# Fewer, longer butterfly operations and a new order of the work beside the matmuls, in a two-part kernel (attention with memory, and a spectral filter)

## The chip, the core and the metric

The kernel runs on one core of one Trainium2 chip, as one program. A core has a matrix engine (PE, with its weight loads shown apart as PEld), a vector engine (DVE), a scalar engine (ACT), a general engine (POOL), and queues that issue transfers between main memory and the core's own memory (SP's queue, POOL's queue). Each engine executes its instructions in the order in which they stand and waits for the others by semaphores. The metric is the device time of one execution in microseconds (us).

## The reference

Two independent computations share the launch and their results are laid side by side.

Part A is attention with a compressive memory: 2048 rows, 576 columns, 32 heads of 18, four segments of 512 rows.

```python
q, k, v = heads(x @ wq), heads(x @ wk), heads(x @ wv)
for s in range(4):                                   # segments
    logits = einsum("hqd,hkd->hqk", q_s, k_s) * 18**-0.5 + causal_mask
    a_dot  = softmax(logits) @ v_s
    a_mem  = (phi(q_s) @ M) / (phi(q_s) @ z + 1e-6)  # phi(t) = t+1 if t>0 else exp(t)
    out_s  = g * a_mem + (1 - g) * a_dot             # g = sigmoid(beta), per head
    M, z   = M + phi(k_s).T @ v_s, z + phi(k_s).sum(rows)
a = concat(out) @ wo
```

Part B filters a real 2048 x 576 array in the frequency domain:

```python
X = rfft2(x)                    # 2048 x 289 complex
b = irfft2(X * (w_r + 1j * w_i))
```

## The kernel before, in words

All matmuls of float32 data are done as three products of rounded halves (high x high, high x low, low x high), so every operand is first split: ACT copies the rounded high half, DVE (or POOL) subtracts it and writes the low half. The program goes through five stages.

1. **Forward transform** (`FFT.forward`, iterations u = 0 to 19, 16 blocks of 128 rows). `prep(u+2)` forms sums and differences of a block (`eo`, DVE, line 125), their high half `eh` (ACT, line 127) and low half `el` (DVE, lines 131 and 132). `f1(u)` transforms along the columns (PE, line 142). `ev0` and `ev1` take the result from PSUM as a high half (ACT, line 146) and a low half (DVE, line 149). `c1(u-3)` transforms 128 points along the rows (PE, line 162, two PSUM tiles of tag "c1", of which there are two), and `evz` copies the result into `Z` one iteration later (ACT, line 153). `Z` is 128 x 4 x 4 x (real, imaginary) x 290: 16 complex rows per partition. Beside it run the splits of the weights of q and k (`load_w`, ACT line 403, DVE lines 405 and 406) and of the first 512 rows of part A's input (`xprep`, DVE lines 432 and 438).
2. **Projections** (`ATT.projections`). Four groups of 13 units: 9 units of q and k (128 output columns each, 14 matmuls of 128x512) and 4 units of v (28 of 128x288). Behind a q or k unit stands a chain: ACT copies the sums to bfloat16 (line 471), DVE subtracts (line 478), ACT copies again (line 482), and PE takes the second part out with a matmul by minus the identity (line 484) that stands in PE's order in the middle of the unit two later. Where phi is wanted, ACT computes exp (line 475) and DVE finishes phi (line 477).
3. **Inverse transform** (`FFT.inverse`, u = 0 to 17): `ysplit` splits the rows of `Z` into `Y` (ACT line 280, POOL or DVE line 281), `i2(u)` transforms along the rows (PE line 296), `T` is taken from PSUM (ACT line 326, DVE line 328), `i3` transforms along the columns (PE line 307). The maxima of the first ten attention heads (`s1`) run between.
4. **Attention** (133 steps), 5. the **last output projection**.

Between the row transforms of stages 1 and 3 the 16 complex rows of each partition go through a 16-point transform as two passes of four-point butterflies, a product with the filter, and the same back. This is all vector work on `Z`, without matmuls: `stage1` (butterfly `bf`, then rotations `tws`), `middle` (butterfly, product with `W`, inverse butterfly, rotations), `last` (inverse butterfly). A butterfly is ten DVE operations (line 206), six on a whole complex row (580 numbers) and four on half of one (290). A rotation is two ACT operations on whole rows (lines 216 and 217) and two DVE operations on halves (lines 222 and 224). The product with the filter is four DVE operations per row, two of them on halves (lines 245 to 252).

These steps stand in a list of generators, and a `Pace` object deals them out: `take(f)` adds f to an account and emits one step for each whole number in it. There are 61 + 165 + 40 = 266 steps. The forward loop takes one per iteration up to u = 13 and two after it (there is nothing to take before u = 7), the projections take a fixed share per unit, with 2.4 times as much in a v unit as in a q or k unit, 0.4 of it ahead of the second step of the earlier unit's chain (the one with line 478) and 0.6 behind it, and ten steps are left for the inverse transform. The order of everything is written out by hand in this way; no scheduler moves instructions.

## Time and profile before

| | |
|---|---|
| three runs | 734.36, 738.96, 740.35 us (median 738.96) |
| the profiled execution's own time | 736.84 us |
| its span, first to last instruction | 735.1 us |
| PE, DVE, ACT, POOL busy | 691.1, 553.4, 457.9, 204.2 us |
| mean granted clock of the matrix engine | 0.994 |

A busy matrix engine is not one at its peak: matmuls overlap, and their ends are modelled, so the distance between the starts of two matmuls says more than their durations. On DVE and ACT, too, an operation's duration is longer than the distance to the start of the next one, since the end of one overlaps the beginning of the next.

### The profile page before, as it was taken

The numbers are of one execution on the slowest core, as the hardware profiler recorded it, in microseconds if no ns is written. First come the engines' busy times: TensorE is split into PE (matmuls) and PEld (weight loads), VectorE is DVE, ScalarE is ACT, GpSimd is POOL, SyncE is SP. The second block draws the span as 40 slices with busy tenths as digits, with TensorE's granted clock in tenths as the row PEclk, the third lists the DMA queues.
The fourth block names the chain that finished last, engine by engine and source line by source line (L and its number), as shares of the span: only waits on it lengthen the run. The fifth ranks groups of instructions, "written<-read, shape, count | busy, mean of one in ns | idle before, by whom it ended". The sixth has DMA issues, their size and how long they took to land.

```text
span 735.1 us, 14249 instructions
## 1 busy us (share of the span) xinstructions
PE 691.1 (94%) x4879; PEld 496.6 (68%) x4879; DVE 553.4 (75%) x1285; ACT 457.9 (62%) x1012; POOL 204.2 (28%) x405
## 2 busy tenths in 40 slices
PE   4998999999999999999999999999999899998897
PEld 4988779879779788899744444443665345653396
DVE  6999879899799788787688878876567575668333
ACT  3666796585585664444487777776566566568521
POOL 2111000100200112565065335462334832325100
PEclk9999999999999999999999999999999899999999
DMA  9884435655373468899547656777456565431231
GB/s 337 264 267 148 144 116 180 197 173 160 133 236 113 169 206 277 213 219 219 179 99 185 168 149 162 179 177 145 117 142 161 142 156 131 108 115 41 70 123 64
DMA packets 83243, 121.04 MB, mean 165 GB/s; under 512 B 11352, under 2 KB 50630, under 8 KB 83036
## 3 DMA queue, kind: packets, MB, share of 16 engines
q1 hardware_dynamic: 76580, 104.11, 49.9%
q0 software_dynamic: 6592, 16.03, 8.0%
q8 instruction: 38, 0.62, 0.3%
q14 instruction: 33, 0.27, 0.1%
HBM read 81.78 MB, written 38.24 MB: 163 GB/s over the span
## 4 chain that ended last, share of the span: by engine, by line
PE 70%; DMA 13%; DVE 7%; ACT 5%; issue 3%; POOL 1%; SPq 1%; ACTq 0%; DVEq 0%; POOLq 0%
PE pj L459 14%; PE pv L709 8%; PE po L829 7%; PE pjv L459 7%; PE s L636 4%; PE i L307 4%; PE i L296 3%; PE s L644 3%; PE s L679 3%; DMA x<-qkD 2%; DMA Ks<-qkD 2%; DMA Qs<-qkD 2%; PE pn L778 2%; PE po L858 2%; PE s L683 2%
## 5 line engine op out<-in xcount | busy, mean ns | idle before, releaser
L640 DVE CUSTOM_DVE_ANT_0 junk<-s,mask 128x512 bf16<-128x512 f32 (+1 forms) x256 | 141.2, 551 | 62.6 <-PE s L636 59.0
L646 DVE TENSOR_REDUCE mx<-s 128x4 f32<-128x512 f32 x128 | 87.9, 687 | 12.0 <-PE s L645 9.2
L692 POOL TENSOR_SCALAR_AFFINE_SELECT P<-P 128x512 f32<-128x512 f32 x116 | 70.0, 634 | 73.9 <-ACT P L680 66.0
L709 PE MATMUL pv<-P,vs 128*32 128x512 f32 (+3 forms) x1024 | 89.3, 445 | 0.3 <-DVE P L694 0.3
L680 ACT ACTIVATE P<-s 128x512 f32<-128x512 f32 x128 | 76.3, 596 | 17.4 <-PE s L679 15.0
L689 ACT ACTIVATE P<-s 128x256 f32<-128x256 f32 x128 | 49.1, 384 | 50.9 <-PE s L688 50.9
L685 ACT ACTIVATE P<-s 128x512 f32<-128x512 f32 x128 | 76.0, 594 | 0.3 <-PE s L684 0.3
L459 PE MATMUL pj<-x,wqkh 128*128 128x512 f32 x162 | 56.5, 409 | 0.0
L206 DVE TENSOR_TENSOR Z<-t,t 128x290 f32<-128x290 f32 (+1 forms) x96 | 48.4, 553 | 0.1
L206 DVE TENSOR_TENSOR t<-Z 128x580 f32<-128x580 f32 x64 | 46.0, 754 | 0.0
L506 POOL MEMSET vt<- 128x32 f32 x16 | 2.3, 161 | 153.8 <-PE pm L516 128.7
L636 PE MATMUL s<-Ks,Qs 108*128 108x512 bf16 (+1 forms) x128 | 42.2, 330 | 0.1
L142 PE MATMUL f<-ftab,eh 128*128 128x290 f32 (+1 forms) x160 | 31.4, 315 | 10.1 <-DMA ftab<-ftab 10.1
L296 PE MATMUL i<-civ,Y 128*128 128x256 f32 (+1 forms) x288 | 38.5, 285 | 1.5 <-POOL Y L281 0.9
L296 PEld LDWEIGHTS i<-civ,Y 128*128 128x128 f32 (+1 forms) x288 | 35.9, 181 | 2.3 <-POOL Y L281 1.3
L709 PEld LDWEIGHTS pv<-P,vs 128*32 128x32 f32 x1024 | 22.4, 109 | 21.9 <-issue 14.6
L645 PE MATMUL s<-tri,idb 128*128 128x256 bf16 x128 | 35.2, 275 | 1.3 <-ACT idb L585 1.3
L307 PE MATMUL i<-itab,T 128*128 128x290 f32 (+1 forms) x224 | 36.0, 309 | 0.0
L459 PE MATMUL pj<-xh,wqkl 128*128 128x512 f32 x90 | 35.5, 395 | 0.0
L459 PE MATMUL pj<-x,wqkl 128*128 128x512 f32 x90 | 35.5, 395 | 0.0
L459 PE MATMUL pj<-xh,wqkh 128*128 128x512 f32 x90 | 35.5, 395 | 0.0
L459 PEld LDWEIGHTS pj<-x,wqkh 128*128 128x128 f32 x162 | 30.4, 188 | 7.2 <-issue 0.6
(211 smaller groups left out, 1830.5 us busy)
## 6 DMA issues: line engine op xcount, KB each, us to landing
qkD<-sp SPq DMA_DIRECT2D x36, 384.0 KB
Ks<-qkD SPq DMA_DIRECT2D x72, 144.0 KB
x<-qkD SPq DMA_DIRECT2D x60, 144.0 KB
Qs<-qkD SPq DMA_DIRECT2D x60, 144.0 KB
xin<-xb SPq DMA_DIRECT2D x16, 384.0 KB
cfw<-cfw POOLq DMA_DIRECT2D x16, 384.0 KB, 4.9
civ<-civ POOLq DMA_DIRECT2D x16, 384.0 KB, 7.6
vs<-vD SPq DMA_DIRECT2D x16, 330.0 KB
```

The costliest lines, as they stand in the source:

```text
L206: v.tensor_tensor(o,a,b,op=op)
L296: nc.tensor.matmul(p[:m,k],Y[i][:,q,c*128:c*128+m],cc[:,hl,o:o+256],start=n==0,stop=n==5)
L307: nc.tensor.matmul(p,x,t,start=n==0,stop=n==6)
L459: s.nc.tensor.matmul(out,a,b,start=i==0,stop=i==len(L)-1)
L636: nc.tensor.matmul(out,Q[:108,h,128*i:128*i+128],K[:108,h,:128*(i+1)],start=True,stop=True)
L640: nc.vector.tensor_tensor_reduce(out=junk[:,:w],in0=src,in1=s.mask[:,512-w:],scale=1.0,scalar=-3.0e38, op0=OP.add,op1=OP.max,accum_out=s.m ...
L646: nc.vector.tensor_reduce(out=s.mx[k][:,hh],in_=pa.rearrange("p (b c) -> p b c",c=128),axis=mybir.AxisListType.X,op=OP.max)
L680: nc.scalar.activation(P[0][:,hh],p0,AF.Exp,scale=SC)
L685: nc.scalar.activation(P[1][:,hh],p1,AF.Exp,scale=SC)
L692: if k<29: nc.gpsimd.affine_select(out=x,in_=x,pattern=pat+[[1,128]],compare_op=OP.is_ge,fill=0.0,base=0,channel_multiplier=-1)
L709: nc.tensor.matmul(s.pvt[32*hh:32*hh+32,128*j:],vt[:,j,19*h:19*h+32],mv[0][:,hh,mv[1]],start=j==0,stop=j==2,skip_group_check=True)
L829: nc.tensor.matmul(ps,a[t][:r,c],b[:r,t,w],start=i==0,stop=i==14)
```

## The change

- A butterfly becomes eight DVE operations, all on 580 numbers: the four on halves become two that write one half each of two rows (`two` makes an output with two pieces) and read the other operand with its two halves in reverse order (`[:,::-1]`).
- A rotation becomes two ACT operations on halves (290 numbers) and one DVE operation on the whole row that multiplies by the cosine and adds (`scalar_tensor_tensor`).
- The product with the filter takes two rows at a time: per pair, four products and two sums or differences, all on 580 numbers.
- The temporaries for these, eight buffers of one row, become four of two rows.
- So there are 44 + 124 + 32 = 200 steps. The forward loop takes none at u = 7, one from 8 to 17 and two at 18 and 19 (14 in all, 19 before); the projections deal with a factor 2.1 for a v unit in the place of 2.4, 0.7 of a unit's share ahead of the chain's step and 0.3 behind it, and leave eight for the inverse transform.
- The weight splits of q and k go column half by column half, and are done in iterations 4 to 8 and 14 to 18 of the forward loop (4 to 13 before). The second row transform of block 14 writes to a PSUM tile of tag "f1".
- In the inverse transform, `ysplit` of blocks 0, 1 and 2 (0 and 1 before) is done during the projections, on DVE and one unit earlier, that of block 3 at the end of u = 0; block 0's `i2` in the place of block 1's uses the PSUM tiles of `i3`; and the two small tables of the attention's mask (`masks`, ACT) stand earlier.

```diff
--- before.py
+++ after.py
@@ -153,8 +153,9 @@
             for r,p in enumerate(C.pop(u)): nc.scalar.copy(s.Z[:,b,a,r],p[:,:FP])
         def c1(u):
             a,b=BORD[u]; x=X.pop(u); cc=cw.pop(u)
+            if u==14: P=pp.tile([128,2,512],F32,name="f1",tag="f1")
             for r in range(2):
-                p=pp.tile([128,512],F32,name="c1",tag="c1")
+                p=pp.tile([128,512],F32,name="c1",tag="c1") if u!=14 else P[:,r]
                 n=0
                 for (i,hl) in ((0,0),(0,1),(1,0)):
                     for q in range(2):
@@ -175,7 +176,7 @@
         for i in range(2):
             for x in p: next(x)
         load(3)
-        s.pace=Pace(61+165+40)
+        s.pace=Pace(44+124+32)
         for u in range(20):
             p=prep(u+2) if u+2<16 else iter(())
             if 0<u<17: ev0(u-1)
@@ -183,26 +184,29 @@
             if u%4==3 and u>6: s.pace.add(s.stage1((u-7)//4))
             next(p,None)
             if 0<u<17: ev1(u-1)
-            if u<14: s.pace.take(1)
+            if 7<u<14: s.pace.take(1)
             next(p,None)
             if u<16: f1(u)
             if u+4<16: load(u+4)
             elif u<18: next(xs,None)
             if 2<u<19: c1(u-3)
             if 0<u<15: loadc(u+1)
-            if 1<u: next(wl,None)
-            if u>13: s.pace.take(2)
+            if 1<u<9 or u>13: next(wl,None)
+            if u>13: s.pace.take(1 if u<18 else 2)
         for _ in wl: pass
         for _ in xs: pass
+    def two(s,a,b):
+
+        l=list(a.ap)
+        return bass.AP(tensor=a.tensor,offset=a.offset,ap=[l[0],[b.offset-a.offset,2],l[1]])
     def bf(s,x,y,inv):
 
         v=s.nc.vector; tp=s.tp
-        t=[tp.tile([128,2,FP],F32,name=f"t{i}",tag="t",bufs=8) for i in range(4)]
+        t=[tp.tile([128,2,2,FP],F32,name=f"t{i}",tag="t",bufs=4) for i in range(2)]; t=[t[i%2][:,i//2] for i in range(4)]
         p,m=(y[1],y[3]) if not inv else (y[3],y[1])
         for o,a,b,op in ((t[0],x[0],x[2],OP.add),(t[1],x[0],x[2],OP.subtract),(t[2],x[1],x[3],OP.add),(t[3],x[1],x[3],OP.subtract),
                          (y[0],t[0],t[2],OP.add),(y[2],t[0],t[2],OP.subtract),
-                         (p[:,0],t[1][:,0],t[3][:,1],OP.add),(p[:,1],t[1][:,1],t[3][:,0],OP.subtract),
-                         (m[:,0],t[1][:,0],t[3][:,1],OP.subtract),(m[:,1],t[1][:,1],t[3][:,0],OP.add)):
+                         (s.two(p[:,0],m[:,1]),t[1],t[3][:,::-1],OP.add),(s.two(m[:,0],p[:,1]),t[1],t[3][:,::-1],OP.subtract)):
             v.tensor_tensor(o,a,b,op=op)
             yield
     def tws(s,L,inv):
@@ -212,16 +216,15 @@
         for i in range(len(L)+1):
             if i<len(L):
                 y,e=L[i]; a=-2*np.pi*e/16*(-1 if inv else 1)
-                t=[s.tp.tile([128,2,FP],F32,name=f"tw{k}",tag="t",bufs=8) for k in range(2)]
-                nc.scalar.activation(t[0],y,AF.Copy,scale=float(np.cos(a)))
-                nc.scalar.activation(t[1],y,AF.Copy,scale=float(np.sin(a)))
-                A.append((y,t))
+                if i%2==0: T=s.tp.tile([128,2,2,FP],F32,name="tw",tag="t",bufs=4)
+                t=T[:,i%2]
+                nc.scalar.activation(t[:,0],y[:,1],AF.Copy,scale=-float(np.sin(a)))
+                nc.scalar.activation(t[:,1],y[:,0],AF.Copy,scale=float(np.sin(a)))
+                A.append((y,t,float(np.cos(a))))
                 if i==0: yield
             if i>0:
-                y,t=A.pop(0)
-                v.tensor_tensor(y[:,0],t[0][:,0],t[1][:,1],op=OP.subtract)
-                yield
-                v.tensor_tensor(y[:,1],t[0][:,1],t[1][:,0],op=OP.add)
+                y,t,c=A.pop(0)
+                v.scalar_tensor_tensor(y,y,c,t,op0=OP.mult,op1=OP.add)
                 yield
     def stage1(s,b):
         x=[s.Z[:,b,a] for a in range(4)]
@@ -240,16 +243,16 @@
             yield from s.bf(x,x,False)
             for d in range(4):
                 W=Ws[4*c+d]
-                t=s.tp.tile([128,2,FP],F32,name="wm",tag="t",bufs=8)
-                t2=s.tp.tile([128,2,FP],F32,name="wm2",tag="t",bufs=8)
-                v.tensor_tensor(t,x[d],W[:,0][:,None,:].to_broadcast([128,2,FP]),op=OP.mult)
+                if d%2==0: t,t2=[s.tp.tile([128,2,2,FP],F32,name=f"wm{k}",tag="t",bufs=4) for k in range(2)]
+                v.tensor_tensor(t[:,d%2],x[d],W[:,0][:,None,:].to_broadcast([128,2,FP]),op=OP.mult)
                 yield
-                v.tensor_tensor(t2,x[d],W[:,1][:,None,:].to_broadcast([128,2,FP]),op=OP.mult)
+                v.tensor_tensor(t2[:,d%2],x[d],W[:,1][:,None,:].to_broadcast([128,2,FP]),op=OP.mult)
                 if 4*c+d+3<16: ld(4*c+d+3)
                 yield
-                v.tensor_tensor(x[d][:,0],t[:,0],t2[:,1],op=OP.subtract)
+                if d%2==0: continue
+                v.tensor_tensor(s.two(x[d-1][:,0],x[d][:,0]),t[:,:,0],t2[:,:,1],op=OP.subtract)
                 yield
-                v.tensor_tensor(x[d][:,1],t[:,1],t2[:,0],op=OP.add)
+                v.tensor_tensor(s.two(x[d-1][:,1],x[d][:,1]),t[:,:,1],t2[:,:,0],op=OP.add)
                 yield
             yield from s.bf(x,x,True)
             yield from s.tws([(x[b],b*c) for b in (2,1,3)],True)
@@ -286,7 +289,7 @@
         T={}; po={}; Yt=s.Yt
         def i2(u,cs):
             Y=Yt[u]; cc=s.civ[u]
-            p=pp.tile([128,len(cs),256],F32,name="i2",tag="i3" if u==1 else "i2")
+            p=pp.tile([128,len(cs),256],F32,name="i2",tag="i3" if u==0 else "i2")
             for k,c in enumerate(cs):
                 n=0
                 for (i,hl) in ((0,0),(0,1),(1,0)):
@@ -324,7 +327,7 @@
                 T[u]=(h,l)
                 p=i2(u,(0,1))
                 nc.scalar.copy(h[:,:2],p)
-                if u+2<16: s.ysplit(u+2)
+                if 1<u<14: s.ysplit(u+2)
                 v.tensor_tensor(l,p,h[:,:2].bitcast(F32),op=OP.subtract)
                 yield
                 flush()
@@ -332,6 +335,7 @@
                 Yt.pop(u); s.civ.pop(u)
                 nc.scalar.copy(h[:99,2],p[:99,0])
                 v.tensor_tensor(h[64:97,2],p[64:97,0],h[64:97,2].bitcast(F32),op=OP.subtract)
+                if u==0: s.ysplit(3)
                 if u+4<16: s.load_civ(u+4)
                 yield
             if u>1:
@@ -407,7 +411,7 @@
     def load_w(s,nm,n,wp,st,w,tag,bufs):
         nc,io=s.nc,s.io
         s.wh[nm]=wp.tile([128,5,n],F32R,name=nm+"h"); s.wl[nm]=wp.tile([128,5,n],F32R,name=nm+"l")
-        J=[(t,o) for t in range(5) for o in range(0,n,w)]; q=[]
+        J=[(t,o) for o in range(0,n,w) for t in range(5)]; q=[]
         for i in range(len(J)+bufs-1):
             if i<len(J):
                 t,o=J[i]
@@ -432,7 +436,7 @@
             eng.tensor_tensor(l,x,h.bitcast(F32),op=OP.subtract)
             s.xl[g,t]=l
         else:
-            l=s.ftp.tile([128,2,FP],F32R,name="xt",tag="t",bufs=8).rearrange("p a b -> p (a b)")[:,:512]
+            l=s.ftp.tile([128,2,2,FP],F32R,name="xt",tag="t",bufs=4).rearrange("p a b c -> p (a b c)")[:,:512]
             nc.scalar.copy(l,x)
             nc.scalar.copy(h[:64],x[:64])
             eng.tensor_tensor(h[64:],x[64:],l.bitcast(F32)[64:],op=OP.subtract)
@@ -539,7 +543,7 @@
             for l in list(live):
                 try: next(l)
                 except StopIteration: live.remove(l)
-        tot=pace.left-10
+        tot=pace.left-8
         for g in range(4):
             if g<3: xq=[s.xprep(g+1,t,(xp,s.x0)[g%2],xp,[128,512],"xst",2) for t in range(5)]
             for i in range(13):
@@ -550,12 +554,12 @@
                 next(lw,None); next(lw,None)
                 if g<3 and i in (4,6,8,10,12): next(xq[(i-4)//2])
                 if g<3 and i in (1,3,5,7,9): next(xq[(i-1)//2])
-                w=tot/(36+16*2.4)*(1.0 if i<9 else 2.4)
+                w=tot/(36+16*2.1)*(1.0 if i<9 else 2.1)
                 advance()
-                pace.take(w*.4)
+                pace.take(w*.7)
                 advance()
                 next(u)
-                pace.take(w*.6)
+                pace.take(w*.3)
                 live.append(u)
         while live: advance()
 
@@ -873,10 +877,10 @@
 
         nc,io=s.nc,s.io
         yield
+        s.masks()
         s.load_v(0)
         q=s.stack_dmas(1,0)+s.stack_dmas(1,1)+s.stack_dmas(2,0)+s.stack_dmas(2,1)+[lambda: s.load_v(1)]+s.stack_dmas(3,1)
         for i in range(2): yield
-        s.masks()
         i=0
         for t in range(10):
             for _ in s.s1(t):
@@ -1065,7 +1069,7 @@
                         F.yp=pool(Ri,"yp",2); F.Yt={}; ci=pool(Ri,"ci")
                         tc.swap_default_side()
                         F.inv_setup(ci)
-                    if g==3 and i>10: F.ysplit(i-11,nc.vector)
+                    if g==3 and i>9: F.ysplit(i-10,nc.vector)
                     if g==3 and i==0: q0.extend(A.stacks0(x0))
                     if g==3 and i>0: q0.pop(0)()
                 q0=[]
```

What this does to the order on the engines is shown at three places. The first is DVE in the forward loop, iteration 11 of 20: `eo`, `el` and `eh` belong to `prep`, `X` is the low half behind `f1`, `Z<-t` is a butterfly step, and `wqkl` a weight split. Before:

```order
L125 TENSOR_TENSOR eo<-xin 128x384 x2
L149 TENSOR_TENSOR X_662<-f_616,X_653 128x580
L206 TENSOR_TENSOR Z<-t_452,t_454 128x580
L131 TENSOR_TENSOR el<-eo,eh 128x512
L132 TENSOR_TENSOR eh<-eo,eh 33x2x128
L405 TENSOR_TENSOR wqkl<-raw,wqkh 128x576
```

With the change (line numbers are those of the changed kernel, three or four higher):

```order
L125 TENSOR_TENSOR eo<-xin 128x384 x2
L149 TENSOR_TENSOR X_652<-f_610,X_643 128x580
L210 TENSOR_TENSOR t_504<-Z 128x580
L131 TENSOR_TENSOR el<-eo,eh 128x512
L132 TENSOR_TENSOR eh<-eo,eh 33x2x128
```

The weight split is gone from this iteration, and from 9, 10, 12 and 13. The second place is DVE at the end of the forward loop and the beginning of the projections (`x` is the split input of part A, `wvl` a weight split of v, and `pj<-pj,sp` the step of the chain behind the first unit of q). Before:

```order
L206 TENSOR_TENSOR t_892<-Z 128x580
L206 TENSOR_TENSOR t_893<-Z 128x580
L432 TENSOR_TENSOR x_828<-xin,x_828 128x512
L438 TENSOR_TENSOR x_828<-xin,xt 64x512
L206 TENSOR_TENSOR t_894<-Z 128x580
L206 TENSOR_TENSOR Z<-t_891,t_893 128x580 x2
L206 TENSOR_TENSOR Z<-t_892,t_894 128x290 x4
L222 TENSOR_TENSOR Z<-tw_1011,tw_1012 128x290
L405 TENSOR_TENSOR wvl<-raw,wvh 128x288
L224 TENSOR_TENSOR Z<-tw_1011,tw_1012 128x290
L478 TENSOR_TENSOR pj<-pj,sp_1036 128x512
```

With the change:

```order
L442 TENSOR_TENSOR x_808<-xin,xt 64x512
L409 TENSOR_TENSOR wqkl<-raw,wqkh 128x576
L210 TENSOR_TENSOR t_907<-Z 128x580
L409 TENSOR_TENSOR wqkl<-raw,wqkh 64x576
L410 TENSOR_TENSOR wqkl<-wqkh 64x576
L210 TENSOR_TENSOR t_906<-Z 128x580
L210 TENSOR_TENSOR t_907<-Z 128x580
L210 TENSOR_TENSOR Z<-t_906 128x580 x2
L210 TENSOR_TENSOR Z<-t_907 128x2x290 x2
L409 TENSOR_TENSOR wvl<-raw,wvh 128x288
L227 SCALAR_TENSOR_TENSOR Z<-Z,tw 128x580
L482 TENSOR_TENSOR pj<-pj,sp_1018 128x512
```

Weight splits of q and k stand here now, and in both orders the chain's step follows the second butterfly and the first rotations. The third place is ACT early in the inverse transform, from the copy of `T` for u = 2 on (`Y<-Z` are the high halves of `ysplit`, `tri` and `idb` the two tables of the mask, `E` the first half of an output). Before:

```order
L326 CAST T_3419<-i_3421 128x512
L280 CAST Y_3435<-Z 128x2x256
L280 CAST Y_3435<-Z 128x2x99
L333 CAST T_3419<-i_3442 99x256
L312 COPY E<-i_3453 128x290
L326 CAST T_3477<-i_3479 128x512
L280 CAST Y_3493<-Z 128x2x256
L280 CAST Y_3493<-Z 128x2x99
L333 CAST T_3477<-i_3501 99x256
L584 CAST tri<-mask 128x128
L585 CAST idb<-ident 128x128
L312 COPY E<-i_3523 128x290
```

With the change, from the copy for u = 1 on:

```order
L329 CAST T_3260<-i_3262 128x512
L336 CAST T_3260<-i_3277 99x256
L329 CAST T_3288<-i_3290 128x512
L283 CAST Y_3304<-Z 128x2x256
L283 CAST Y_3304<-Z 128x2x99
L336 CAST T_3288<-i_3311 99x256
L588 CAST tri<-mask 128x128
L589 CAST idb<-ident 128x128
L315 COPY E<-i_3322 128x290
L329 CAST T_3348<-i_3350 128x512
L283 CAST Y_3364<-Z 128x2x256
L283 CAST Y_3364<-Z 128x2x99
```

The tables stand ahead of the first `E` now, one copy of `T` and one `ysplit` earlier, and u = 1 has no `ysplit` any more.

## The prediction

> **What bounds the kernel now.** I read the page's first part, then the stretches of the stages, then the waits of the matrix engine, and last its neighbours' rows where it waits.
>
> ```profile
> PE 691.1 (94%) x4879; PEld 496.6 (68%) x4879; DVE 553.4 (75%) x1285; ACT 457.9 (62%) x1012; POOL 204.2 (28%) x405
> ```
>
> The change adds no matmul and removes none. What it can gain is therefore time in which PE waits for others. The stretches (length, then busy time of PE, PEld, DVE, ACT, POOL, then clock and transfers) show where that is:
>
> ```profile
> 38.00:76.00 38.00, 33.56 (x234) 31.49 (x233) 36.94 (x63) 23.30 (x49) 3.97 (x11) 1.00 0.63 191
> 76.00:284.00 208.00, 206.09 (x1169) 174.77 (x1168) 179.56 (x338) 141.35 (x278) 14.27 (x62) 1.00 0.54 177
> 284.00:300.00 16.00, 13.22 (x101) 11.96 (x99) 10.09 (x19) 8.64 (x23) 8.94 (x15) 1.00 0.74 205
> 300.00:357.00 57.00, 56.95 (x448) 54.01 (x446) 45.53 (x111) 25.02 (x61) 27.53 (x40) 1.00 0.88 213
> ```
>
> From 38 to 76 us, the second half of the forward loop, DVE is busy for 36.9 of 38 us and PE waits: DVE sets the time there. From 76 to 284, the projections, PE is idle for 1.9 us of 208, with DVE idle for 28.4. From 284 to 300 PE loses 2.8 us at the start of the inverse transform, then nothing to 357. The attention behind it is touched by no edit. So there are three places, worth at most about 4.4 + 1.9 + 2.8 us of visible idle time and what restarting PE adds.
>
> **First place, the forward loop.** PE's rows (start, busy time, group; in brackets its idle time and who ended it):
>
> ```profile
> 31.21 1.78 PE L162 MATMUL c<-X,cfw 128*128 128x290 f32 x12
> 34.72 1.79 PE L162 MATMUL c<-X,cfw 128*128 128x290 f32 x12
> 38.34 1.88 PE L162 MATMUL c<-X,cfw 128*128 128x290 f32 x12
> 46.59 1.89 PE L162 MATMUL c<-X,cfw 128*128 128x290 f32 x12 [0.35 <-ACT Z L153]
> 63.94 1.88 PE L162 MATMUL c<-X,cfw 128*128 128x290 f32 x12 [1.22 <-ACT Z L153]
> 70.11 3.48 PE L162 MATMUL c<-X,cfw 128*128 128x290 f32 x24 [0.77 <-ACT Z L153]
> 74.32 1.88 PE L162 MATMUL c<-X,cfw 128*128 128x290 f32 x12 [0.73 <-ACT Z L153]
> 76.04 0.63 PE L459 MATMUL pj<-x,wqkh 128*128 128x512 f32 x2
> ```
>
> Undisturbed, an iteration of PE takes 34.72 - 31.21 = 3.51 us. The wait is put down to ACT's copies into `Z`. But ACT itself waits for DVE, in this cycle of iteration 9:
>
> ```profile
> 43.17 1.02 DVE L125 TENSOR_TENSOR eo<-xin 128x384 f32<-128x384 f32 x2
> 44.11 0.75 DVE L149 TENSOR_TENSOR X<-f,X 128x580 fp32r<-128x580 f32 x1
> 44.78 0.75 DVE L206 TENSOR_TENSOR t<-Z 128x580 f32<-128x580 f32 x1
> 45.45 0.68 DVE L131 TENSOR_TENSOR el<-eo,eh 128x512 fp32r<-128x512 f32 x1
> ...
> 46.62 0.76 DVE L405 TENSOR_TENSOR wqkl<-raw,wqkh 128x576 fp32r<-128x576 f32 x1
> 47.30 1.02 DVE L125 TENSOR_TENSOR eo<-xin 128x384 f32<-128x384 f32 x2
> ...
> 44.28 0.84 ACT L127 CAST eh<-eo 128x768 fp32r<-128x768 f32 x1 [1.57 <-DVE eo L125]
> 45.02 0.67 ACT L403 CAST wqkh<-raw 128x576 fp32r<-128x576 f32 x1
> 45.60 0.64 ACT L146 CAST X<-f 128x580 fp32r<-128x580 f32 x1
> 46.13 0.70 ACT L153 COPY Z<-c 128x290 f32<-128x290 f32 x2
> ```
>
> DVE's cycle is 47.30 - 43.17 = 4.13 us, and ACT's `eh` waits for its `eo`. The weight split takes 0.68 us of DVE's cycle (46.62 to 47.30) and 0.58 of ACT's path to `Z` (45.02 to 45.60). Without it, in iterations 9 to 13, DVE needs 4.13 - 0.68 = 3.45 us, less than PE's 3.51: PE sets the pace there. One heavy cycle is left: iteration 8 now has the split of the last tile, which is two operations on DVE, so 4.13 + 0.7 = 4.8 us, for which PE waits an estimated 1.2 us.
>
> From the second transform at 38.34 to the first projection PE then needs seven iterations, 7 x 3.51 = 24.6, four more second transforms (the row at 70.11 shows two in 3.48), 7.0, and the 1.2: 32.8 us. Before it took 76.04 - 38.34 = 37.7. **Gain 4.9 us.** For that the waits at the end of the loop (1.22, 0.77, 0.73) must go too. There the splits return, one per iteration from u = 14, but `prep` is over by then; block 14 gets a PSUM tile that was free; and two butterfly steps per iteration become one. ACT's work of such an iteration (one X copy, two Z copies, an input and a weight copy, about 0.55 + 0.6 + 0.5 + 0.6) is 2.3 us, which covers u = 14 and 15 (3.51 of PE each) and is tight at 16 and 17 (1.7 each). Bounds: 3.2 us if the waits of the last two rows stay, 5.9 if the heavy cycle costs nothing.
>
> What it costs is debt on DVE. At u = 14 it begins about 60.9, and until the projections it has three X steps, five input and five weight splits (one double) and eight butterfly steps, all near 0.68: 15 us, to 76, when PE began the projections at about 71. Before, it was level.
>
> **Second place, the projections.** They must absorb 5 us of that debt. First the size of the vector work, from its rows in the projections and two neighbouring starts:
>
> ```profile
> L206 DVE TENSOR_TENSOR t<-Z 128x580 f32<-128x580 f32 x51 | 36.4, 755 | 0.0
> L206 DVE TENSOR_TENSOR Z<-t,t 128x290 f32<-128x290 f32 x52 | 21.0, 453 | 0.1
> L477 DVE SCALAR_TENSOR_TENSOR ex<-pj,ex 128x512 f32<-128x512 f32 x26 | 17.9, 688 | 16.7 <-ACT ex L475 16.6
> PE pj L484 <- ACT sp L482: 1.8, 3, 1.0
> 74.41 0.76 DVE L206 TENSOR_TENSOR t<-Z 128x580 f32<-128x580 f32 x1
> 75.09 2.91 DVE L206 TENSOR_TENSOR Z<-t,t 128x580 f32<-128x580 f32 x6
> ```
>
> An operation on 580 numbers lasts 0.755 us, but the next starts 75.09 - 74.41 = 0.68 later. The six of the last row are two such and four on 290: (2.91 - 0.453 - 2 x 0.68)/3 = 0.37 apart. Two on 290 replaced by one on 580 so save 0.06 us, not the 0.15 that the durations suggest. With 64 halves in butterflies, 36 in rotations and 32 in products halved in number, 66 x 0.06 = **4 us of DVE** over the whole program. [...]
>
> Two things have no row: an operand read with its halves reversed, an output in two distant pieces. Rows nearest: `eo` and `el` walk pieces of larger tiles, `el` at 0.68 for 512. I take the plain price; the other end is a rate cut in half, +0.6 for each of some 44 in the projections.
>
> Per q or k unit (3.49 of PE) the change deals (200 - 14 - 8)/(36 + 16 x 2.1) = 2.56 steps of 0.68, 1.7 us; before 237/(36 + 16 x 2.4) = 3.19 of about 0.5, 1.6. With line 478 (0.6) and two weight splits of v (0.74) a unit has 3.1 us, so in the first units DVE repays 0.4 each. The first matmul of line 484 is due at 71 + 2.5 x 3.26 = 79.1; DVE, at 76 + two steps, a weight split, a rotation and the chain's own (1.36 + 0.37 + 0.68 + 0.6), is done at 79.0, and ACT's copy behind it at 79.6 to 80: PE waits 0.5 to 0.9. Against it the 1.8 us of waits for line 482 should shrink, since ACT's rotations, which stand ahead of it, go from 692 ns to the size of a copy into `Z` (two in 0.70 us above):
>
> ```profile
> L216 ACT ACTIVATE tw<-Z 128x580 f32<-128x580 f32 x18 | 12.4, 692 | 3.0 <-DVE Z L206 3.0
> ```
>
> Later the 28.4 us of idle DVE pay the rest, 16.7 of them waits for exp that 0.7 of the share, dealt ahead of line 477, fills. **Gain 0.9 us**, between a loss of 3 and a gain of 2.
>
> **Third place, the inverse transform.**
>
> ```profile
> 289.40 0.75 PE L296 MATMUL i<-civ,Y 128*128 128x256 f32 x4 [0.34 <-ACT Y L280]
> 290.80 0.38 PE L296 MATMUL i<-civ,Y 128*128 128x256 f32 x1 [0.65 <-POOL Y L281]
> 291.45 1.81 PE L296 MATMUL i<-civ,Y 128*128 128x256 f32 x13 [0.27 <-POOL Y L281]
> 298.81 0.28 PE L645 MATMUL s<-tri,idb 128*128 128x256 bf16 x1 [1.30 <-ACT idb L585]
> 287.38 0.70 ACT L509 COPY vt<-pjv 128x288 f32<-128x288 f32 x2 [2.91 <-DMA vD<-vt]
> 289.65 0.59 ACT L326 CAST T<-i 128x512 fp32r<-128x512 f32 x1
> 294.28 0.40 ACT L312 COPY E<-i 128x290 f32<-128x290 f32 x1
> ```
>
> The tables come two ACT groups earlier, near 294: the 1.30 goes, with 0.1 for restarting. The earlier `ysplit` removes the waits for `Y` (0.34 + 0.65 + 0.27), but `i2` of u = 2 now follows u = 1 into the same PSUM tiles and waits for that one's copy (289.65) and DVE's subtraction, about 291.0; ACT is held until 287.38 by a transfer, which no edit moves. So 0.2 of it. **Gain 1.6 us**; 2.9 at most. At the other end, ACT would stand at the first table until its transfer, issued near 288.6, has landed; four neighbours took 4.8 us, so 293.4, in time. At the 9.9 that the chain shows for `vD<-vt` it would be 298.5, a loss of 4 us there.
>
> ```profile
> civ<-civ POOLq DMA_DIRECT2D x4, 384.0 KB, 4.8
> 277.38 9.91 DMA vD<-vt
> ```
>
> **Sum.** 4.9 + 0.9 + 1.6 = 7.4 us from the profiled execution's own 736.84 (span 735.1 and 1.7 around it): 729.4. The three runs average 737.9, 1.1 above it (their median 2.1); with that 730.5. I forecast 730.
>
> **Rivals.**
> - *The debt is paid by PE.* The chain behind a unit stays late through the first group, whose units 4 to 6 have more DVE work (line 477, an input split) than PE time. For it: only 0.4 us a unit is repaid. Against: DVE is idle for 7 us in each group. The full loss of 3 us and no gain gives 729.4 + 3.9, about 733 to 734.
> - *The end of the loop still waits*, as ACT is the one that is late there: 1.7 less in the first place and nothing in the second, 732 to 733.
> - *Reversed or split rows run at less than half rate* (the slower side). Place: the two last steps of each butterfly and the two sums of a product. At half rate, 44 x 0.6 = 26 us stand against 28 us of idle DVE less 5 of debt, and PE loses about 3. From (23 + 7.4)/44 = 0.7 us extra per operation on, PE loses more than was won; at three times the price, 44 x 1.36 = 60, it is some 37 more than 729.4, about 766.
> - *The clock.* In the attention PE waits for late transfers, and then the granted clock is halved:
>
> ```profile
> 579.40:586.20 6.80, 6.50 (x25) 2.39 (x25) 4.33 (x14) 2.88 (x7) 6.76 (x9) 0.50 0.48 109
> ```
>
> Such a stretch costs half of 6.8, 3.4 us; none gives 726, two 733. [...] The change only shifts when those transfers meet.
>
> **How the numbers follow.** Forecast (727 to 732.5) 0.58; debt 0.15; late end of the loop 0.08; clock 0.12, half of it each way; reversed rows 0.07. The range, 723.5 to 738.5, takes in all but the last and tails. A measurement of this kernel can tell about 1% (7.4 us) from no change, so faster by over 1% means under 731.6: most of the forecast's chance and half of the clock's, 0.53. Slower by over 1%, above 746.3: 0.07. The rest, 0.40.
>
> **What would show it.** Right: DVE's cycle of iterations 9 to 13 near 3.45, PE's projections starting near 71, the first line-484 matmul late by under 1 us, no wait for `idb`. Wrong: merged operations over 0.8 us, PE idle for more than 4 us in the projections, or ACT idle ahead of the first table.

## The result

| | before | changed |
|---|---|---|
| median of the timed runs | 736.80 us (20 runs) | 733.86 us (20 runs) |
| profiled execution, own time (span) | 736.84 (735.1) | 735.77 (734.1) |

The ratio is 0.9948, with a 95% interval of 0.9933 to 0.9962: 3.8 us faster (2.8 to 4.9), half of the 7.4 us that the prediction's sum gives. A second comparison (below) gave 0.9938, 0.9912 to 0.9964. Ratios go by runs in the chip's usual, fast state: of the 210 runs of the four comparisons below three were slow, one of them of the changed kernel with 1117.01 us at a mean granted clock of 0.561, and are left out. The page of the changed kernel, and its stretches, with the same edges as those shown of before:

```profile
PE 692.6 (94%) x4879; PEld 496.4 (68%) x4879; DVE 548.0 (75%) x1221; ACT 449.8 (61%) x1012; POOL 203.4 (28%) x403
38.00:76.00 38.00, 36.53 (x248) 34.58 (x248) 36.61 (x61) 23.99 (x52) 4.04 (x11) 1.00 0.66 199
76.00:284.00 208.00, 205.26 (x1180) 174.44 (x1179) 178.84 (x285) 134.34 (x280) 15.43 (x65) 1.00 0.54 177
284.00:300.00 16.00, 13.80 (x108) 13.06 (x107) 10.92 (x22) 8.78 (x23) 8.68 (x12) 1.00 0.82 209
300.00:357.00 57.00, 56.22 (x435) 52.67 (x434) 41.88 (x103) 24.12 (x59) 25.74 (x38) 1.00 0.82 207
```

From 38 to 76 PE is busy for 36.5 us, 3 more than before. From 76 to 284 it is idle for 2.7 us where it was 1.9. In the two stretches of the inverse transform PE is idle for 3.0 us, 0.2 more than before, though the chosen edges cut other work by now. A better measure is the distance between starts of matmuls. PE's rows at the borders of the stages (before's first two rows ahead of those of the changed kernel; before's projections start at 76.04, as the prediction shows):

```profile
9.20 0.82 PE L142 MATMUL f<-ftab,eh 128*128 128x290 f32 x2 [9.20 <-DMA ftab<-ftab]
10.95 0.85 PE L142 MATMUL f<-ftab,eh 128*128 128x290 f32 x2 [0.92 <-DMA ftab<-ftab]
...
284.53 4.53 PE L296 MATMUL i<-civ,Y 128*128 128x256 f32 x36 [0.22 <-ACT vt L509]
...
370.44 1.06 PE L709 MATMUL pv<-P,vs 128*32 128x512 f32 x8
```

```profile
7.71 0.82 PE L142 MATMUL f<-ftab,eh 128*128 128x290 f32 x2 [7.71 <-DMA ftab<-ftab]
9.35 0.85 PE L142 MATMUL f<-ftab,eh 128*128 128x290 f32 x2 [0.81 <-DMA ftab<-ftab]
...
70.67 0.63 PE L463 MATMUL pj<-x,wqkh 128*128 128x512 f32 x2
...
279.93 1.33 PE L299 MATMUL i<-civ,Y 128*128 128x256 f32 x9 [0.30 <-ACT vt L513]
...
365.56 0.64 PE L713 MATMUL pv<-P,vs 128*32 128x512 f32 x4
```

The same four distances were read in every profile. "Forward" runs from the first `f` to the first `pj` matmul, less PE's further waits for `ftab` in it; "projections" to the first `i` matmul; "inverse" to the first `pv` matmul; "rest" to the end of the span. "Waits" are PE's for the chain (line 484 before, 488 changed). All in us:

| kernel (its section below) | forward | projections | inverse | sum | waits | rest |
|---|---|---|---|---|---|---|
| before | 65.9 | 208.5 | 85.9 | 360.3 | 1.8 | 364.7 |
| changed | 62.1 | 209.3 | 85.6 | 357.0 | 2.4 | 368.5 |
| changed, again | 62.0 | 208.8 | 83.6 | 354.5 | 2.4 | 365.2 |
| splits undone | 64.7 | 206.9 | 84.5 | 356.1 | 0.7 | 364.7 |
| splits alone | 62.4 | 211.1 | 85.7 | 359.3 | 4.2 | 364.1 |
| vector operations alone | 65.8 | 206.5 | 85.6 | 357.9 | 0.5 | 365.8 |
| dealing undone | 62.2 | 207.8 | 85.1 | 355.1 | 1.1 | 362.9 |
| inverse undone | 61.9 | 209.4 | 87.8 | 359.1 | 2.4 | 361.7 |
| block 1 in i3's tiles | 62.9 | 209.1 | 83.6 | 355.6 | 2.4 | 365.9 |
| v's rows into pk | 61.9 | 208.8 | 88.8 | 359.6 | 2.4 | 363.7 |
| first combination | 60.6 | 207.8 | 84.3 | 352.7 | 1.3 | 362.6 |
| the same, again | 60.7 | 207.9 | 84.3 | 352.8 | 1.3 | 366.0 |
| second combination | 60.8 | 207.5 | 85.6 | 354.0 | 1.0 | 366.3 |
| without pk's buffer | 60.5 | 208.7 | 84.6 | 353.7 | 1.0 | 362.1 |

In the first profile the change gave 3.8 in the forward loop, lost 0.8 in the projections and gave 0.3 in the inverse transform; the attention, whose instructions are the same, then took 3.9 more.

### The profile page after: what moved, and what is told of

Read it like the earlier page. It is cut to its first block, busy times and chain, and to the rows that moved or that the text cites. A ratio compares the mean times of both kernels' runs of the same rounds, so it can differ in the third digit from the quotient of the medians.

```text
span 734.1 us, 14182 instructions
## 1 busy us (share of the span) xinstructions
PE 692.6 (94%) x4879; PEld 496.4 (68%) x4879; DVE 548.0 (75%) x1221; ACT 449.8 (61%) x1012; POOL 203.4 (28%) x403
## 4 chain that ended last, share of the span: by engine, by line
PE 71%; DMA 10%; DVE 7%; ACT 6%; issue 3%; POOL 1%; SPq 0%; ACTq 0%; DVEq 0%; POOLq 0%
PE pj L463 12%; PE pv L713 9%; PE po L833 7%; PE pjv L463 7%; PE s L640 5%; PE s L648 3%; PE s L683 3%; PE i L299 3%; DMA yb<-yout 3%; PE i L310 3%; PE s L687 2%; PE pn L782 2%; PE po L862 2%; DMA Qs<-mts 2%; PE pm L520 2%
## 5 line engine op out<-in xcount | busy, mean ns | idle before, releaser
L210 DVE TENSOR_TENSOR Z<-t 128x580 f32<-128x580 f32 x64 | 45.8, 755 | 0.1
```

What stands on the lines that cost most here:

```text
L210: v.tensor_tensor(o,a,b,op=op)
```

## The experiments

Each comparison has the kernel before beside it on the same chip.

**The changed kernel again: is the loss in the attention its own?**

> The changed kernel once more. In its first profile the attention, whose instructions nobody changed, took 327.7 us from the first to the last pv matmul; five other profiles with the same instructions there show 320.8 to 325.0. Theory (chance): the attention comes out at 321 to 326 here, with another number of stretches at half clock, the stages ahead of it are again 3.3 us shorter in sum than before, and the time is 3 to 4 us below the kernel before. Rival (an earlier start makes the attention's transfers meet worse): about 327 again, with a wait for Ks of over 2 us near 473.

Measured: 732.12 us median beside 737.83 of before, ratio 0.9938 (0.9912 to 0.9964). The rest took 365.2 us, against 364.7 before, and over all fourteen profiles 361.7 to 368.5: the 368.5 was chance. What varies there are waits for transfers and the clock. The first profile waits 2.7 us for `Ks` (before's 1.7), and its clock is at half for 13.65 us of the attention, before's for 6.83 (see the last section). So the gain has to be looked for in the stages ahead.

**The places of the weight splits, undone and alone.**

```diff
-            if 1<u<9 or u>13: next(wl,None)
+            if 1<u: next(wl,None)
```

> The changed kernel with one part undone: the weight splits of q and k stand in iterations 4 to 13 of the forward loop again. Theory (the forward gain is DVE's shorter cycle in iterations 9 to 13): their cycle goes from 3.45 back to 4.13, 5 x 0.62 = 3.1 us of PE lost, while the heavy cycle of iteration 8 (0.9) and the wait at the end of the loop (0.8) go: the first projection matmul 1.0 to 2.0 us later, counted from the first matmul of the program. But five splits less stand on DVE there, so the waits at line 488 (2.4 us) should shrink by about 1: in all 0 to 1.5 us slower than the changed kernel. Rival (the gain comes from having fewer steps at the end of the loop, not from where the splits stand): the first projection matmul moves by less than 0.5 us and the total falls by the 1 us of the waits.

The other way round, in the kernel before, with block 14's tile and the order of the tiles:

```diff
-            if 1<u: next(wl,None)
+            if 1<u<9 or u>13: next(wl,None)
```

> The kernel before with the new places of the weight splits alone (iterations 4 to 8 and 14 to 18, column half by column half, and block 14's second transform in a tile of f1). Theory (a loan: what PE wins in iterations 9 to 13 it loses in the projections, as undoing this part in the changed kernel showed, 2.6 longer in the forward loop and 2.3 shorter in the projections): the forward loop 1.5 to 2.6 us shorter, the projections 1.5 to 2.6 longer, by longer waits at line 484; in all within 1 us of the kernel before. Rival (the forecast's first place): 3.2 us or more faster.

Undone: ratio 0.9960 (0.9935 to 0.9986) to before; against the two profiles of the changed kernel the forward loop is 2.5 to 2.6 us longer and the projections 1.9 to 2.3 shorter. Alone: 0.9977 (0.9955 to 1.0000), 3.5 shorter and 2.6 longer than before. PE's waits for the chain in both, the undone one first:

```profile
PE pj L488 <- ACT sp L486: 0.7, 1, 0.7
```

```profile
PE pj L485 <- ACT sp L483: 4.2, 4, 1.6
```

The theory of a loan holds: of some 3 us that the new places win in the forward loop, two thirds and more are paid back in the projections, most of it in waits of the first group (3.7 us there alone, 1.2 before; 0.7 undone, 2.4 in the changed kernel). Net they are worth 0.2 to 0.9 us.

**The vector operations alone.** All of the butterfly, rotation and product code, the temporaries and the step counts in the kernel before; splits, dealing factors and inverse transform as before.

> The kernel before with the new vector operations alone (200 steps, the same 14 of them in the forward loop as in the changed kernel; everything else where it stood). Theory 1 (operations bring only what DVE saves where PE waits for it): iterations 9 to 13 keep one step and one split each, so the cycle stays 4.1 us; 4 steps less at the end of the loop, about 2 us of DVE, bring 1 us at most; the waits at line 484 fall from 1.8 to about 1: 1 to 2 us faster than the kernel before. Theory 2 (they are half of the change): 3 us or more faster. In both DVE's busy time falls by 5.4 us, as in the changed kernel, and the two-piece and reversed operations last 0.755 us.

Measured: 0.9987 (0.9961 to 1.0013), median 734.61 beside 737.79; the total alone hardly tells the theories apart. Up to the inverse transform the stages give 2.1 us, of which 1.95 lies in the projections; the waits go from 1.8 to 0.5. That is nearer to theory 1, though of the 1 us that it allowed the forward loop only 0.1 came. DVE's busy time fell by 4.8 us (553.4 to 548.6, with 66 instructions less), not by 5.4. DVE's groups in the changed kernel, by form:

```profile
L210 DVE TENSOR_TENSOR t<-Z 128x580 f32<-128x580 f32 x64 | 46.1, 755 | 0.1
L210 DVE TENSOR_TENSOR Z<-t 128x580 f32<-128x580 f32 x64 | 45.8, 755 | 0.1
L227 DVE SCALAR_TENSOR_TENSOR Z<-Z,tw 128x580 f32<-128x580 f32 x18 | 13.4, 755 | 5.3 <-ACT tw L222 5.3
L253 DVE TENSOR_TENSOR Z<-wm,wm 128x580 f32<-128x580 f32 x8 | 6.1, 759 | 0.2
```

The second row holds the operations with a reversed operand and a two-piece output (half of the 64), the fourth two-piece ones: 755 and 759 ns, as the plain ones. The distances between starts say the same, in the last four operations of one butterfly, two plain and two of the new form:

```profile
74.47 2.78 DVE L210 TENSOR_TENSOR Z<-t 128x580 f32<-128x580 f32 x4
```

They are (2.78 - 0.755)/3 = 0.68 apart, as plain ones were before. The price that had no row before is the plain price.

**The dealing in the projections undone** (2.4, 0.4 ahead and 0.6 behind, in the place of 2.1, 0.7 and 0.3).

```diff
-                w=tot/(36+16*2.1)*(1.0 if i<9 else 2.1)
+                w=tot/(36+16*2.4)*(1.0 if i<9 else 2.4)
-                pace.take(w*.7)
+                pace.take(w*.4)
-                pace.take(w*.3)
+                pace.take(w*.6)
```

> The changed kernel with the dealing of the projections undone: factor 2.4 for a v unit, 0.4 of a share ahead of the chain's step and 0.6 behind it. Theory (the waits at line 488 come from vector work dealt ahead of the chain): 2.39 steps for a q or k unit in the place of 2.56, of which 0.96 stand ahead and not 1.79, so the chain's step comes 0.6 us earlier: the 2.4 us of waits fall to about 1 and the projections take 1.0 to 1.5 us less. Rival (the waits come from the splits that the forward loop left over, and the dealing is worth the forecast's 16.7 us of waits for exp): the waits stay at 2 or more, or PE waits elsewhere, and the projections take as long or 1 us more.

Measured: 730.82 us beside 737.83, ratio 0.9923 (0.9895 to 0.9951), below the changed kernel of the same comparison (732.12), with intervals that overlap. The projections took 1.0 to 1.4 us less and the waits 1.1 in the place of 2.4: the theory. The new dealing costs about 1 us. The waits are the firmer figure: they are 2.4 in all five profiles with this dealing and these splits, while the projections of two versions below, which differ by one buffer, lie 1.1 us apart (207.5 and 208.7). How it comes about, at the first matmul of line 488 in the changed kernel, then with the old dealing:

```profile
77.53 0.76 DVE L227 SCALAR_TENSOR_TENSOR Z<-Z,tw 128x580 f32<-128x580 f32 x1
78.21 0.69 DVE L482 TENSOR_TENSOR pj<-pj,sp 128x512 f32<-128x512 f32 x1
...
79.30 0.57 ACT L486 CAST sp<-pj 128x512 bf16<-128x512 f32 x1
...
79.92 0.38 PE L488 MATMUL pj<-sp,nid 128*128 128x512 bf16 x1 [0.93 <-ACT sp L486]
```

```profile
79.23 0.70 DVE L482 TENSOR_TENSOR pj<-pj,sp 128x512 f32<-128x512 f32 x1
...
79.83 0.76 DVE L227 SCALAR_TENSOR_TENSOR Z<-Z,tw 128x580 f32<-128x580 f32 x1
...
80.95 0.38 PE L488 MATMUL pj<-sp,nid 128*128 128x512 bf16 x1 [0.26 <-ACT sp L486]
```

In the changed kernel a rotation stands on DVE ahead of the chain's step (line 482), and with the old dealing behind it. From that step on the two are alike: ACT's copy of line 486 starts 1.09 us later in both (79.30 here, 80.32 with the old dealing), behind two weight copies each time. So the wait differs by the 0.68 of the rotation (0.93 and 0.26).

**The inverse transform's part undone, and one tile of it.**

```diff
-                if 1<u<14: s.ysplit(u+2)
+                if u+2<16: s.ysplit(u+2)
-                if u==0: s.ysplit(3)
-                    if g==3 and i>9: F.ysplit(i-10,nc.vector)
+                    if g==3 and i>10: F.ysplit(i-11,nc.vector)
```

The tiles of `i3` go to block 1 as in the second diff below, and `masks` stands where it stood before.

> The changed kernel with the inverse transform's part undone: splits of blocks 0 and 1 alone ahead of it, block 1 in the tiles of i3, the mask's tables back behind the first two steps. Theory A (the forecast's third term): 1.6 us slower. Theory B (the two traces: from the first transform of block 0 to the first matmul of the attention 85.9 us before and 85.6 after): 0.3 us slower, the waits for Y (0.34, 0.65, 0.27) and for idb (1.30) return and the 2.20 for T of block 1 goes.

Measured: 0.9973 (0.9941 to 1.0005). From block 0 to the attention 87.8 us, but a stretch of that ran at half clock (0.50, the third number from the end):

```profile
288.90:292.31 3.41, 3.41 (x18) 3.41 (x17) 1.12 (x2) 1.74 (x4) 3.25 (x4) 0.50 0.85 206
```

That costs an estimated half of 3.41, 1.7 us; without it 86.1, against 85.6 and 83.6 in the two profiles of the changed kernel. So this part is worth 0.5 to 2.5 us, and the expectations were too close to be told apart. All four waits came back as expected (1.3 for `idb`, 0.5, 0.6 and 0.3 for `Y`).

```diff
-            p=pp.tile([128,len(cs),256],F32,name="i2",tag="i3" if u==0 else "i2")
+            p=pp.tile([128,len(cs),256],F32,name="i2",tag="i3" if u==1 else "i2")
```

> The changed kernel with block 1, and not block 0, in the PSUM tiles of i3. Block 2 then follows into tiles that block 0 has left, and its split is already done. Theory: the wait of 2.20 us for T at the start of the inverse transform falls to 0.2 and nothing else is late: 2.0 us faster than the changed kernel. Rival (the wait only moves, to i3 of block 0, which now needs the tiles of block 1, and to Y of block 3 on POOL): 0 to 0.8 us faster. Either way the start of the attention shows it; what the attention then makes of it is open.

Measured: 0.9912 (0.9883 to 0.9942); the wait for `T` was 0.6 and the inverse transform 83.6 us. That looked like the theory, until the changed kernel's second profile showed a wait of 0.76 and 83.6 too, without the edit. What differs between its two profiles is ACT (first profile, then second; third, PE's and ACT's rows with the edit):

```profile
282.96 0.70 ACT L513 COPY vt<-pjv 128x288 f32<-128x288 f32 x2 [3.09 <-DMA vD<-vt]
283.56 0.59 ACT L329 CAST T<-i 128x512 fp32r<-128x512 f32 x1
...
286.65 0.62 PE L299 MATMUL i<-civ,Y 128*128 128x256 f32 x3 [2.20 <-DVE T L331]
```

```profile
281.75 0.71 ACT L513 COPY vt<-pjv 128x288 f32<-128x288 f32 x2 [1.94 <-DMA vD<-vt]
282.36 0.59 ACT L329 CAST T<-i 128x512 fp32r<-128x512 f32 x1
...
285.47 0.74 PE L299 MATMUL i<-civ,Y 128*128 128x256 f32 x4 [0.76 <-DVE T L331]
```

```profile
282.42 4.52 PE L299 MATMUL i<-civ,Y 128*128 128x256 f32 x36
...
286.19 0.59 ACT L329 CAST T<-i 128x512 fp32r<-128x512 f32 x1
...
287.56 2.40 PE L299 MATMUL i<-civ,Y 128*128 128x256 f32 x18 [0.62 <-DVE T L331]
```

Counted from the first `i` matmul (279.93 and 280.30), the first copy into `T` comes 3.63 and 2.06 us later, and PE waits 1.43 and 1.30 less than that. But the edit does act: with it the copy came as late as in the first profile (3.77), and yet PE waited only 0.62. PE goes on 1.37 us after the copy, without the edit 3.09 and 3.11, as block 2 needs the tiles of block 0 and no longer those of block 1. So at the same hold of ACT the edit takes 1.6 us off the wait, near the theory's 2.0; where ACT comes early, as in the second profile, at most 0.8 is left to win. On the total it isn't shown: the interval overlaps both of the changed kernel's.

**A buffer for v's rows**, so that ACT need not wait for the transfer `vD<-vt`:

```diff
+        if g==3 and tb==0: s.vk=tp.tile([128,4,576],F32,name="pk",bufs=1).rearrange("p a b -> p (a b)")
-        vt=tp.tile([128,622],F32,name="vt")
+        vt=s.vk[:,622*tb-622:622*tb] if g==3 and tb>0 else tp.tile([128,622],F32,name="vt")
```

> The changed kernel with one buffer more for v's rows: in the last group of the projections v units 2 to 4 write into the space of pk, which nobody needs there, so that ACT's copies vt no longer wait for the transfer vD<-vt of two units earlier. Theory (this wait sets the start of the inverse transform: the wait of PE for T of block 1 was 2.20, 0.76, 2.13, 0.62 and 1.44 us in five profiles, longer where ACT was held longer): ACT is idle at line 513 (514 here) for PE alone, the wait for T falls to 0.3 to 0.7 in every profile, and from the first transform of block 0 to the first tri matmul PE needs 11.5 to 11.9 us (13.25 and 11.68 in the two profiles of the changed kernel): 0 to 1.5 us faster in one profile, some 0.8 us on the mean. Rival (the PSUM tiles set it, as block 2 follows block 1 into them): the wait stays over 1 us.

Measured: 0.9980 (0.9951 to 1.0009), the inverse transform 88.8 us. ACT's copies were indeed free, but its first copy into `T` now waited, for the transfers out of `pk`:

```profile
285.33 0.59 ACT L329 CAST T<-i 128x512 fp32r<-128x512 f32 x1 [4.37 <-DMA vD<-pk]
```

PE's rows of the same profile:

```profile
280.36 0.87 PE L299 MATMUL i<-civ,Y 128*128 128x256 f32 x6
...
288.37 1.01 PE L299 MATMUL i<-civ,Y 128*128 128x256 f32 x3 [3.58 <-DVE T L331]
```

The copy is 4.97 after the first `i` matmul, and PE's wait again 1.4 less. Behind this wait the clock was halved too (third number from the end):

```profile
287.04:293.87 6.83, 5.50 (x25) 5.50 (x26) 2.30 (x5) 2.95 (x9) 3.76 (x5) 0.50 0.43 135
```

Of the 88.8 us an estimated 3.4, half of 6.83, are this; without them 85.4, no more than in the changed kernel's first profile. The remedy failed, as the wait only moved; that the end of v's transfers sets this wait is shown by it. Why `T` depends on that space wasn't tried: the pool of `T` opens where that of the projections closed, which would explain it.

**Versions meant to beat both.**

```diff
-            if u==14: P=pp.tile([128,2,512],F32,name="f1",tag="f1")
+            if u in (13,15): P=pp.tile([128,2,512],F32,name="f1",tag="f1")
-                p=pp.tile([128,512],F32,name="c1",tag="c1") if u!=14 else P[:,r]
+                p=pp.tile([128,512],F32,name="c1",tag="c1") if u not in (13,15) else P[:,r]
-            if 7<u<14: s.pace.take(1)
+            if 8<u<14: s.pace.take(1)
-                w=tot/(36+16*2.1)*(1.0 if i<9 else 2.1)
+                w=tot/(9*.6+27+16*2.1)*((1.0 if g else .6) if i<9 else 2.1)
```

and block 1 in the tiles of `i3`:

> A version meant to beat both: the changed kernel with block 1 in the tiles of i3 (a 2.2 us wait that fell to 0.6), no butterfly step in the heavy iteration 8 of the forward loop, the row transforms of blocks 13 and 15, not 14, in tiles of f1 (the wait of 0.77 at the end of the loop), and 0.6 of the share for the q and k units of group 0 (the waits at line 488, 2.4 us in that group). If each wait goes: forward loop 1 to 1.5 us shorter, projections 1.5 us shorter, inverse transform 2 us shorter, 4.5 to 5 us in all below the changed kernel. If the debt only moves to the next groups: 2 to 3 us.

> The first combined version once more (block 1 in the tiles of i3, no butterfly step in iteration 8, blocks 13 and 15 in tiles of f1, 0.6 of the share in group 0). Its stages should repeat within 0.6 us: forward loop 60.6, projections 207.8; from the first block of the inverse transform to the attention 83.5 to 85.5, by how long v's transfers hold ACT; 6 to 8.5 us below the kernel before. If the first comparison was luck: 4 us, as for the changed kernel.

Measured: 729.78 us, ratio 0.9901 (0.9872 to 0.9931), and 730.32, 0.9917 (0.9898 to 0.9936). The forward loop is 1.4 to 1.6 us shorter than in the changed kernel, the projections 1.0 to 1.4, both repeating within 0.2 us. The inverse transform stays at 84.3, as DVE now has leftover steps ahead of `T` there: its subtraction starts 2.52 us after ACT's copy (283.08 and 280.56), with block 1's edit alone 0.63, and PE goes on 3.26 after the copy, so that the edit's gain is lost. It is about 2.5 us below the changed kernel (0.9948 and 0.9938), with intervals that overlap in part.

With the old dealing and the buffer for v's rows, and then without the buffer:

> All that helped together: the version of the last comparison (block 1 in the tiles of i3; no butterfly step in iteration 8; blocks 13 and 15 in tiles of f1; 0.6 of the share in group 0), with the dealing of the kernel before (factor 2.4, 0.4 of a share ahead of the chain's step), and with the buffer for v's rows. Expected by stages: forward loop 60.5 us as in that version, projections 206.5 to 207.3 (207.8 there; undoing the dealing gave 1.0 to 1.4 in the changed kernel, of which group 0's smaller share may have had a part), from the first block of the inverse transform to the attention 83.0 to 83.8 us (84.3 there): 1.5 to 2 us below that version, 8 to 9.5 below the kernel before. If waits at line 488 have another cause: 0 to 0.5 below it.

> The last version without the buffer in pk's space. The buffer moved ACT's wait from its copies vt to its first copy into T, which then waited 5.30 us for a transfer out of pk. Theory (ACT's hold by v's transfers sets the start of the inverse transform, wherever it stands): without the buffer the first copy into T comes about 1 us earlier and the wait for T falls from 2.95 to 0.6 to 2.2; projections 207.5; 1 us below the last version. Rival (the tiles of PSUM set it): the wait stays near 3.

Measured: 0.9911 (0.9875 to 0.9946) and 0.9932 (0.9908 to 0.9957). Without the buffer the wait for `T` fell from 2.95 to 1.83, as expected; the ratio didn't follow, and the projections took 208.7 us, not 207.5. Neither beats the first combination: with group 0 spared already, the old dealing brings nothing that these runs can tell.

## Why the prediction was right in sign and half of the size

The time, 733.86, lies in the range and 3.9 us above the forecast. By stages, 1.0 to 1.1 us of what was promised is missing in the first place, 1.3 to 1.7 in the second, and in the third 1.3 by the first profile and nothing by the second.

**First place, 4.9 us forecast, 3.8 measured.** The mechanism is as told. DVE's cycle of a free iteration is 52.81 - 49.35 = 3.46, forecast 3.45; the heavy one is 42.44 - 37.46 = 4.98, forecast 4.8:

```profile
37.46 1.02 DVE L125 TENSOR_TENSOR eo<-xin 128x384 f32<-128x384 f32 x2
...
42.44 1.03 DVE L125 TENSOR_TENSOR eo<-xin 128x384 f32<-128x384 f32 x2
...
49.35 1.02 DVE L125 TENSOR_TENSOR eo<-xin 128x384 f32<-128x384 f32 x2
...
52.81 1.03 DVE L125 TENSOR_TENSOR eo<-xin 128x384 f32<-128x384 f32 x2
```

The term was mis-sized by its neighbours, which PE's rows show:

```profile
37.04 1.89 PE L163 MATMUL c<-X,cfw 128*128 128x290 f32 x12
40.87 1.88 PE L163 MATMUL c<-X,cfw 128*128 128x290 f32 x12
45.29 1.87 PE L163 MATMUL c<-X,cfw 128*128 128x290 f32 x12 [0.65 <-ACT Z L153]
49.03 1.87 PE L163 MATMUL c<-X,cfw 128*128 128x290 f32 x12
...
65.74 1.87 PE L163 MATMUL c<-X,cfw 128*128 128x290 f32 x12 [0.77 <-ACT Z L153]
```

Seven iterations were taken at 3.51. The first is 3.83, as DVE's cycle just ahead of it (33.63 to 37.46, with a split and no butterfly step); before, PE's rows were 3.51 apart beside such cycles, as PE lagged behind DVE there. Behind the heavy one (4.42) another takes 3.74. Of the three waits at the end of the loop one stayed (0.77). From the row at 37.04 to 70.67 are 33.6 us, forecast 32.8; the other 0.3 was lost ahead of it. (By the forecast's own terms the bound with a heavy cycle that costs nothing is 4.9 + 1.2 = 6.1, not 5.9.)

**Second place, a gain of 0.9 forecast, a loss of 0.4 to 0.8 measured: the step that failed.** The first wait was right (due at 79.1, 0.5 to 0.9 late; measured 0.93 at 79.92). But the forecast let the debt end there and the old 1.8 us shrink. Of those, 1.2 stood in the first group and 0.5 in the third; the 0.5 went, but the first group has two more waits of 0.7 to 0.8, and 2.4 in all:

```profile
PE pj L488 <- ACT sp L486: 2.4, 3, 0.9
```

The parts taken apart show the three terms that stood behind the one number: the moved splits cost 1.9 to 2.6 here (forecast: absorbed), the vector operations give 1.95 (forecast: 4 us of DVE, of which most would pay the debt), and the new dealing costs 1.0 to 1.4 where the forecast counted it as a help. Added up they would be a loss of about 1 to 2 us, more than was measured; each is read from single profiles, and how they act on one another stays open. This is the first rival, "the debt is paid by PE", for a part: its loss was 3, and about a quarter of that or less came. That the measured time is its 733 to 734 is in part luck, as over a microsecond was missing in the first place too and, in the first profile, as much again in the third.

**Third place, 1.6 forecast, 0.3 and 2.3 in two profiles.** The wait behind block 1's `T` was named and placed (6.5 us after block 0's first matmul; 6.72 and 5.17 measured), and the wait for `idb` is gone. Taken as 1.1 us of the old 1.26, it was 2.20 and 0.76. What wasn't seen is that the hold of ACT by v's transfer, taken as fixed, varies by over a microsecond from run to run (ACT waited 3.09 and 1.94 us for `vD<-vt` in the two profiles), and that block 1 and not block 0 in the tiles of `i3` would have shortened it.

**The attention, 0 forecast.** Right on the mean (364.6 over the thirteen other profiles, 364.7 in that of before) and wrong in the profile, by 3.9; the rival of the clock had the price right, an estimated 3.4 for the 6.8 us more at half clock. Late transfers do stand ahead of before's stretch (PE waited 1.10 us for DVE at 575.47, which had waited 2.56 us for `ux<-uD`) and ahead of the changed kernel's first (2.73 us for `Ks<-qkD`, up to 473.32), but not of its last, at 671.48, where PE waited 0.96 us for DVE and 0.84 for ACT.

**Reversed and split rows**: plain price (755 and 759 ns beside 755), so that this rival falls. With the vector operations alone DVE's busy time fell by 4.8 us for 66 instructions, 0.07 each where the forecast had 0.06. (In the changed kernel it is 5.4 for 64, as two operations of `ysplit` come to DVE from POOL.)

## What to carry to other kernels

Work taken away from beside one stage that an engine paces was in this kernel mostly lent, as the next stage started with that engine in debt: cost the debt until it is repaid, unit by unit, not only at its first wait. A gain in the middle of a long program is judged by distances between starts of the bounding engine's instructions, stage by stage: in five profiles with the same forward loop and, but for one buffer, the same projections, each of these lay within 1 us, while the total of one kernel moved by 8.

## What the runs showed of the hardware

In the profile of before and the first of the changed kernel, the program's start and end aside, PE's half-clock stretches last 3.41 us or twice that: before's 6.83 from 579.37, the changed kernel's 3.41 from 473.51, 6.83 from 575.91 and 3.41 from 671.48. The changed kernel's lie on a grid: the second and third start 102.40 and 197.97 us after the first, 30 and 58 times 3.413 us. Each stretch follows a window of 3.41 us in which PE was idle for a good part: it was busy for 1.61 us ahead of before's and for 0.69, 1.76 and 2.17 ahead of these. The last columns of these stretches are the granted clock, the transfers' share and GB/s; the changed kernel, then before:

```profile
470.10:473.51 3.41, 0.69 (x5) 0.26 (x4) 1.44 (x6) 0.56 (x3) 1.68 (x3) 1.00 0.62 142
473.51:476.92 3.41, 3.41 (x16) 1.05 (x15) 1.39 (x3) 1.70 (x3) 0.46 (x1) 0.50 0.59 156
...
668.07:671.48 3.41, 2.17 (x14) 0.93 (x17) 3.38 (x6) 2.88 (x8) 0.61 (x1) 1.00 0.03 5
671.48:674.90 3.42, 3.42 (x11) 0.71 (x4) 2.74 (x5) 1.34 (x3) 0.00 (x0) 0.50 0.02 5
```

```profile
671.53:674.94 3.41, 2.16 (x16) 0.64 (x13) 3.38 (x7) 3.32 (x9) 0.61 (x1) 1.00 0.04 5
674.94:678.36 3.42, 3.42 (x21) 1.19 (x18) 2.53 (x5) 2.76 (x7) 0.00 (x0) 1.00 0.02 5
```

With windows of 3.413 us laid through these stretches, of the two profiles' full-clock windows the two with PE busy for less than half were followed by half clock, between 0.5 and 0.65 it was two of ten, and above that none of 400. The two kernels have the same waits near 670, of at most 0.96 us each, and busy times of 2.17 and 2.16; one lost an estimated 1.7 us to it, half of 3.41, the other nothing. So half clock followed in this case on a window whose waits are all under 1 us. At half clock, the windows with 3.08 (before) and 2.73 us (changed) busy, the first halves of the two stretches of 6.83, were followed by another, the four with 3.41 were not. Over the 207 runs by which the ratios of the four comparisons go, each 3.41 us at half clock (from the mean granted clock of the run) goes with 1.73 us more (+-0.20), and that accounts for some 60% of the variance between runs of the same kernel. The pair above shows that PE's busy time in a window and its longest wait don't decide alone whether half clock follows; what else does, and what makes up the rest of the variance, isn't shown.
